# Delta-rule attention and two MLPs on one core: the second inverse gets its own buffers, the first is shared between GpSimdE and VectorE

## The chip, the cores and the metric

The kernel runs on one core of one Trainium2 chip. The metric is the device time of one execution in microseconds (us). The engines are named as in the profile: PE is TensorE (matmul), PEld its weight loads, DVE is VectorE, ACT is ScalarE, POOL is GpSimdE, and SP is SyncE, which in this kernel issues the DMAs.

## The reference, cut to what matters

```python
# attention: B, H, S, D = 4, 8, 768, 48; k_n = k / (norm(k) + 1e-6)
for t in range(S):
    y[:, :, t] = einsum('bhd,bhde->bhe', q[:, :, t], state)
    v_old = einsum('bhde,bhd->bhe', state, k_n[:, :, t])
    state = state + beta[t] * einsum('bhd,bhe->bhde', k_n[:, :, t], v[:, :, t] - v_old)
x = y laid out as (B*S, H*D) = (3072, 384)
# first MLP (384 -> 2048 -> 384), weights in float64
h = x @ w_in;  P = a0 + a1*h + a2*h^2 + a3*h^3;  Q = 1 + |b0|*|h| + |b1|*h^2
x = (P / (Q + 1e-6)) @ w_out
# second MLP, other weights
out = (max(x @ w_in2, 0)**2) @ w_out2
```

## The kernel before, in words

**Attention.** The 768 positions are cut into 12 chunks of 64. A step is one chunk of one batch (4 pairs of heads), and 8 steps (2 chunks x 4 batches) are a group: 6 groups. Inside a chunk the recurrence is solved with the inverse of a unit lower triangular matrix built from K^T K. For a whole group this is done at once, with 128 partitions that hold 32x32 blocks: the two diagonal blocks of each 64x64 matrix are inverted row by row (one multiply into `tmp`, one subtraction from `Tt`, for each of 31 values of s), and two small matmul stages (`m1`, `m2`) make the off-diagonal block. `Gb` holds the scaled K^T K, `Tt` the growing inverse, `TT` the finished 64x64 blocks, `TN` the transposed copies for the matmuls, `nbr` and `nrm` what comes from the norms and beta.

Groups 2 to 5 are inverted on POOL in rows of 32 (`st1` L504, `st2` L508), while the first MLP runs. Groups 0 and 1 take another way in the kernel before: 16x16 blocks on DVE (`st16`, L495 and L497, 15 values of s), and then a merge from 16 to 32 on PE (`ma` L565, `mb` L576, `mc` L587, with `me` L569 on DVE), through `Nb`, `Eb`, `DN`, `ident` and `half`. All groups share one `Gb` and one `Tt`, and K^T K of group 1 goes through DRAM (`gs`) to come back as `Gb`.

A step of the attention (L702, L761, L762) needs its mask on POOL (L740, one for each half of a tile `X`), copies on ACT and additions to the state on DVE.

**The MLPs.** They work on 512 tokens (two chunks) at a time: i = 0 to 5 in the first layer, then 6 again in the second. For each i there are 16 blocks j of the hidden layer: 9 matmuls with `Aw[j]` (L902, split into a high and a low part), the function on ACT, POOL (L922) and DVE, and 3 matmuls with `Bw[j]` (L938). The first i of layer 1 needs group 0 of the attention; group i+1 is done inside the time of i. The first layer's weights arrive as float64, 768 KB for each j, and are turned into float32 on ACT (L844) and DVE (L845, L846, L849, L851); ACT (L860) and POOL (L861) make the high and low parts of `Aw[j]`. DVE's and POOL's parts are once for each j.

**The order.** A planner (`Plan`) takes all tasks with assumed durations, due times and buffer pools, plays them through several times and keeps the best order. Each engine then executes its own list strictly in that order: an instruction that waits holds up all that stands behind it on its engine. `T0` is the planned time of the first MLP matmul, `inv_due` when the inverses are due. Matmuls on a tile `ones` fill planned gaps of PE. In the kernel before, SP issues all DMAs, weights too.

Of the kernel before, what the change touches and what calls it, by code (L numbers as in the profile page):

```python
# [48 lines left out]
class Plan:  # L49
# [13 lines left out]
    def add(self, eng, dur, fn, r=(), w=(), due=0.0, lock=0, alloc=None, free=(), kb=0, after=(), iss=0.35, nb=0.0):  # L63
# [179 lines left out]
def kernel(ctx, tc, kT, kS, qT, kn, vn, beta, par_in, w1, w2, outT):  # L243
# [117 lines left out]
    def eye():  # L361
        P_.memset(ident, 0.0)
        for o in range(0, 128, 32):
            P_.affine_select(ident[o:o + 32], ident[o:o + 32], pattern=[[1, 32]], base=0, channel_multiplier=-1,
                             compare_op=ALU.not_equal, fill=1.0)
    add("POOL", 1.0, eye, w=["ident"], due=15)

    def halves():
        P_.memset(half, 1.0)
        for o in range(0, 128, 32):  # L370
            P_.affine_select(half[o:o + 32], half[o:o + 32], pattern=[[0, 1]], base=-16, channel_multiplier=1, compare_op=ALU.is_ge, fill=0.0)
    add("POOL", 0.6, halves, w=["half"], due=5)
    add("POOL", 1.0, lambda: P_.memset(Nb, 0.0), w=[("N", o) for o in range(0, 128, 32)], due=3)
# [16 lines left out]
    def inv_due(g):  # L390
# [3 lines left out]
        if g == 1:  # L394
            return T0 - 10, T0 + 20
# [56 lines left out]
    def attention(g):  # L452
        d0, d1 = inv_due(g)
        if g:
            for n in range(8, 24) if g == 1 else ():
                dn = 8 + 1.5 * n if n < 16 else GD + 2 * (n - 16)
                gload(n, dn, 1.5 * n - 2 if n < 16 else GN + 2 * (n - 16))
                add("PE", 0.6, lambda n=n: [M.matmul(*y, start=True, stop=True) for y in gram(n)], r=[("kg", n)], w=[("G", n)], due=dn,  # L458
                    alloc=(("att", "h") if n < 16 else ("att",), ("G", n)), free=[("kg", n)])
# [625 lines left out]
```

## Time and profile before

| | before |
|---|---|
| median of 3 runs | 1114.44 us (1114.34 to 1118.63) |
| the profiled execution's own time | 1113.5 us |
| its span | 1111.8 us |
| PE busy | 1062.5 us (96%) |
| DVE / ACT / POOL busy | 693.9 / 658.6 / 396.9 us |
| mean granted clock of PE | 0.965 |

The span is what the profiler's rows cover; the execution's own time is 1.7 us longer. Rows give start, duration, engine, line and operation, and in brackets idle time of that engine just before and what ended it. A clock of 1.00 is PE at 2.4 GHz, 0.50 at 1.2 GHz.

### The profile page before, as it was taken

What the parts mean: (1) busy time and instruction counts of PE and PEld (TensorE: products, weight loads), DVE (VectorE), ACT (ScalarE), POOL (GpSimd) and SP (SyncE); (2) the same over time, 40 slices, a digit from 0 to 9 for tenths busy, and PEclk for the clock granted to TensorE, in tenths of its full rate; (3) what the DMA queues carried; (4) which work ended last, traced back from release to release, by engine and by line L of the source; (5) the groups of instructions that cost most, each with busy time, mean ns of one, the idle gap of its engine ahead of it and who ended that gap; (6) DMA issues with size and microseconds to landing.
All of it is one profiled execution on the core that took longest, in us unless ns stands there. A gap on an engine that the chain in (4) does not pass through costs nothing.

```text
span 1111.8 us, 24492 instructions
## 1 busy us (share of the span) xinstructions
PE 1062.5 (96%) x10014; PEld 757.8 (68%) x10014; DVE 693.9 (62%) x1116; ACT 658.6 (59%) x1193; POOL 396.9 (36%) x540
## 2 busy tenths in 40 slices
PE   6688999999999999999999899999999999999998
PEld 5576665556665666666666455688888888888887
DVE  4658988896667667766677599995333333333432
ACT  5265877877767777777878588754324242333422
POOL 6104699468528843972233153552000000000000
PEclk7577999999999999999999999999999999999999
DMA  7465336820640263033010220720001010000000
GB/s 234 103 174 160 70 99 191 219 67 23 158 93 33 74 154 83 13 95 83 29 28 12 90 85 29 240 101 29 29 0 57 1 48 10 1 29 1 29 1 29
DMA packets 116064, 83.48 MB, mean 75 GB/s; under 512 B 83568, under 2 KB 101104, under 8 KB 115952
## 3 DMA queue, kind: packets, MB, share of 16 engines
q1 hardware_dynamic: 115952, 81.92, 26.2%
q8 instruction: 79, 1.29, 0.5%
q14 instruction: 33, 0.27, 0.1%
HBM read 62.88 MB, written 17.83 MB: 73 GB/s over the span
## 4 chain that ended last, share of the span: by engine, by line
PE 84%; DVE 6%; POOL 4%; issue 3%; ACT 2%; DMA 1%; SPq 0%; POOLq 0%; ACTq 0%; DVEq 0%
PE bank L902 34%; PE bank L938 20%; PE bank L964 6%; PE bank L962 6%; PE bank L963 6%; PE bank L702 6%; PE bank L761 2%; POOL tmp L504 1%; POOL Tt L508 1%; PE bank L613 1%; PE bank L625 1%; DVE tmp L495 1%; POOL mem L922 1%; PE bank L458 1%; DMA mem<-in_w_dram 1%
## 5 line engine op out<-in xcount | busy, mean ns | idle before, releaser
L902 PE MATMUL bank<-xh,A 128*128 128x512 f32 x1152 | 360.1, 394 | 3.0 <-POOL A L861 3.0
L938 PE MATMUL bank<-mem,B 128*128 128x512 f32 x576 | 278.0, 615 | 1.3 <-DVE mem L929 1.3
L902 PEld LDWEIGHTS bank<-xh,A 128*128 128x128 f32 x1152 | 218.4, 190 | 62.6 <-issue 13.0
L902 PE MATMUL bank<-xl,A 128*128 128x512 f32 x576 | 254.2, 441 | 5.2 <-DVE mem L929 5.2
L922 POOL TENSOR_TENSOR mem<-mem 128x512 f32<-128x512 f32 x96 | 127.6, 1329 | 200.5 <-ACT mem L920 199.7
L938 PEld LDWEIGHTS bank<-mem,B 128*128 128x128 f32 x576 | 105.1, 192 | 98.8 <-issue 84.6
L950 DVE SCALAR_TENSOR_TENSOR mem<-bank,mem 128x512 f32<-128x512 f32 x96 | 66.1, 689 | 151.4 <-ACT mem L949 151.3
L949 ACT ACTIVATE mem<-bank 128x512 f32<-128x512 f32 x96 | 57.4, 598 | 152.8 <-PE bank L902 152.5
L902 PEld LDWEIGHTS bank<-xl,A 128*128 128x128 f32 x576 | 109.3, 190 | 43.6 <-issue 12.9
L964 PE MATMUL bank<-gh,C 128*128 128x512 f32 x288 | 113.9, 395 | 0.0
L962 PE MATMUL bank<-gl,C 128*128 128x512 f32 x288 | 113.6, 394 | 0.0
L963 PE MATMUL bank<-gh,C 128*128 128x512 f32 x288 | 112.1, 389 | 0.0
L953 DVE TENSOR_TENSOR gl<-mem,gh 128x512 fp32r<-128x512 f32 x96 | 71.5, 745 | 63.4 <-ACT gh L952 63.2
L952 ACT CAST gh<-mem 128x512 fp32r<-128x512 f32 x96 | 59.6, 620 | 74.9 <-DVE mem L950 61.9
L927 DVE SCALAR_TENSOR_TENSOR mem<-mem,par,bank 128x512 f32<-128x512 f32 x96 | 71.3, 743 | 51.6 <-ACT bank L926 51.4
L923 DVE TENSOR_TENSOR mem<-bank,mem 128x512 f32<-128x512 f32 x96 | 65.8, 686 | 39.8 <-ACT mem L347 38.7
L925 ACT ACTIVATE mem<-mem,par 128x512 f32<-128x512 f32 x96 | 69.4, 723 | 34.2 <-POOL mem L922 33.6
L920 ACT ACTIVATE mem<-mem,par 128x512 f32<-128x512 f32 x96 | 78.0, 813 | 2.5
L919 ACT ACTIVATE mem<-bank 128x512 f32<-128x512 f32 x96 | 56.9, 592 | 37.7 <-PE bank L902 37.0
L347 ACT COPY X<-bank 64x256 f32<-64x256 f32 (+1 forms) x189 | 63.7, 337 | 19.6 <-DVE vn L745 10.5
L924 DVE SCALAR_TENSOR_TENSOR mem<-mem,par,bank 128x512 f32<-128x512 f32 x96 | 71.6, 746 | 3.4 <-ACT mem L919 0.7
L504 POOL TENSOR_TENSOR tmp<-Gb,Tt 128x31 f32<-128x31 f32 (+15 forms) x124 | 67.0, 540 | 16.9 <-DVE Tt L489 8.5
(124 smaller groups left out, 1557.5 us busy)
## 6 DMA issues: line engine op xcount, KB each, us to landing
raw<-in_w_dram SPq DMA_DIRECT2D x18, 768.0 KB, 4.8
B<-in_w_dram SPq DMA_DIRECT2D x10, 768.0 KB, 4.8
kTg<-in_kS_dram SPq DMA_DIRECT2D x40, 128.0 KB, 2.8
gs<-Gs SPq DMA_DIRECT2D x40, 128.0 KB, 2.9
kTc<-in_kT_dram SPq DMA_DIRECT2D x40, 128.0 KB, 2.1
X<-in_qT_dram SPq DMA_DIRECT2D x96, 48.0 KB, 2.8
kn<-in_kn_dram SPq DMA_DIRECT2D x12, 384.0 KB, 4.0
vn<-in_vn_dram SPq DMA_DIRECT2D x12, 384.0 KB, 3.6
```

The lines of the kernel that those rows point to most:

```text
L504: P_.tensor_tensor(tv, _mid(Gb[:, s, s + 1:32], [128, a, b]), Tt[:, 0:a, s:s + 1].to_broadcast([128, a, b]), op=ALU.mult)
L902: M.matmul(h, a, b, start=(k == 0 and m == 0), stop=(k == NK - 1 and m == 2))
L920: add("ACT", 0.83, lambda: A_.activation(b(), a(), AF.Identity, bias=s(4), scale=s(5)), r=[ak, "par"], w=[bk], due=due + 3.3, alloc=(("b", ...
L922: add("POOL", 1.32, lambda: P_.tensor_tensor(b(), b(), a(), op=ALU.mult), r=[ak], w=[bk], due=due + 4.2, lock=1)
L924: add("DVE", 0.75, lambda: V.scalar_tensor_tensor(c(), c(), s(1), h(), op0=ALU.add, op1=ALU.mult), r=[hk, "par"], w=[ck], due=due + 6.3)
L925: add("ACT", 0.72, lambda: A_.activation(a(), b(), AF.Ln, bias=s(6)), r=[bk, "par6"], w=[ak], due=due + 6)
L927: add("DVE", 0.75, lambda: V.scalar_tensor_tensor(c(), c(), s(0), h(), op0=ALU.add, op1=ALU.mult), r=[hk, "par"], w=[ck], due=due + 8)
L938: M.matmul(acc[d], Bw[j][:, 128 * d:128 * d + 128], slot[gk], start=(j == 0), stop=(j == NJ - 1))
L953: add("DVE", 0.72, lambda: V.tensor_tensor(gl(), b(), gh(), op=ALU.subtract), r=[bk, gk, "late"], w=[lk], due=due + 5, lock=1, alloc=(("gl ...
L962: M.matmul(acc[d], wh, gl, start=(j == 0), stop=False)
L963: M.matmul(acc[d], wl, gh, start=False, stop=False)
L964: M.matmul(acc[d], wh, gh, start=False, stop=(j == NJ - 1))
```

## The change

Groups 0 and 1 are no longer done in blocks of 16 with a merge. Both use the row-by-row inverse of 32. For group 0, rows 0 to 2 of each block are computed on POOL and rows 3 to 31 on DVE, each with its own `tmp` (rows don't depend on each other). Group 1 is inverted wholly on POOL, as groups 2 to 5 are, and its result goes through DRAM as theirs does. There are two sets of `Gb` and `Tt`, so the second inverse doesn't wait for the buffers of the first. K^T K for steps 8 to 31 is done ahead of the first MLP (8 to 23 before), with four buffers each for load and store in place of two. The first layer's weights are asked for by ACT (`A_.dma_start`) in place of SP, and the planner starts them at 24 us and spaces them by 4.5 us. `T0` goes from 88 to 78.

```diff
-T0, U1, U2 = 88.0, 6.0, 4.15
+T0, U1, U2 = 78.0, 6.0, 4.15
-STEP0, STEP1, INV0, INV1 = 40, 25, -90, -10
-GD, GN = T0 + 10, 60
+STEP0, STEP1, INV0, INV1, LAZY = 40, 25, -100, -10, 0
+NEARLY, ROW0, WNB, WSTEP = 32, 3, 24, 4.5
+GD = 28
...
-    tmp = at.tile([128, 256], F32, name="tmp")
+    Gbs, Tts = ([at.tile([128, 32, 32], F32, name=f"{x}{i}") for i in range(2)] for x in ("Gb", "Tt"))
+    tmps = {x: at.tile([128, 256], F32, name=f"tmp{x}") for x in ("DVE", "POOL")}
...
-    tiles(at, "kTg", 2, [128, NP, C])
-    tiles(at, "Gs", 2, [128, NP, C])
+    tiles(at, "kTg", 4, [128, NP, C])
+    tiles(at, "Gs", 4, [128, NP, C])
...
         if g == 1:
-            return T0 - 10, T0 + 20
+            return 25, T0
...
-        either(0.35, 0.3, o1, r=[key], w=[("Dg", n)], due=n, free=[key])
+        add("ACT", 0.28, lambda f=o1: A_.copy(*f()), r=[key], w=[("Dg", n)], due=n, free=[key])
         for o in (32, 96):
-            either(0.33, 0.3, lambda o=o, f=o2: f(o), r=[key], w=[("TN", o)], due=n + 8, free=[key])
+            add("DVE", 0.28, lambda o=o, f=o2: V.tensor_copy(*f(o)), r=[key], w=[("G21", o)], due=n + 2, free=[key])
...
-            for n in range(8, 24) if g == 1 else ():
+            for n in range(8, NEARLY) if g == 1 else ():
...
-        for s in range(15 if g < 2 else 0):
...
-            add("DVE", 0.42 + 4.0e-3 * a * b, st16, r=GB, w=["Tt", "tmp"], due=d1, lock=1)
-        for s in range(31 if g > 1 else 0):
+        for s in range(31):
+            b = 31 - s
+            for E_, eng, lo, hi in ((V, "DVE", ROW0, s + 1), (P_, "POOL", 0, min(ROW0, s + 1))) if g == 0 else ((P_, "POOL", 0, s + 1),):
...
+                    E_.tensor_tensor(tv, _mid(Gb[:, s, s + 1:32], [128, a, b]), Tt[:, lo:hi, s:s + 1].to_broadcast([128, a, b]), op=ALU.mult)
...
+                    E_.tensor_tensor(Tt[:, lo:hi, s + 1:32], Tt[:, lo:hi, s + 1:32], tv, op=ALU.subtract)
...
-        for hf in range(2 if g < 2 else 0):
-            ka, kb, kc = ("mA", g, hf), ("mB", g, hf), ("mC", g, hf)
...
-            m = n + 16 if 0 < g < NG - 2 else None
+            m = n + 16 if NEARLY <= n + 16 < NSS else None
...
+        if l == 1:
+            add("ACT", 0.3, lambda: A_.dma_start(raw(rk), src[j]), w=[(rk, 0)], due=2 + 4.5 * j, alloc=None if e else (("raw",), rk), nb=WNB + WSTEP * j)
```

The order on POOL moves most. In the kernel before, this stands on POOL from the masks of steps 4 to 7 to the first function of the MLP (`X` masks, `vn` values times norms, `A_79` to `A_84` the low parts of `Aw[0]` to `Aw[5]`):

```order
L740 AFFINE_SELECT X_109<-X_109 64x4x64 x2
L657 TENSOR_TENSOR vn_130<-vn_130,nT_126 128x768
L539 MEMSET TT_112 32x32x32 x2
L740 AFFINE_SELECT X_110<-X_110 64x4x64 x2
L475 MEMSET Tt 128x1024
L861 TENSOR_TENSOR A_82<-mem,A_82 128x384
L657 TENSOR_TENSOR vn_131<-vn_131,nT_126 128x768
L861 TENSOR_TENSOR A_83<-raw_103,A_83 128x384
L922 TENSOR_TENSOR mem<-mem 128x512 x3
```

`A_79` to `A_81` stand ahead of this piece, and no inverse does. In the changed kernel the same place reads (`Gb_115`, `Tt_117`: group 1's own buffers):

```order
L485 TENSOR_TENSOR tmpPOOL<-Gb_115,Tt_117 128x87
L667 AFFINE_SELECT X_110<-X_110 64x4x64 x2
L489 TENSOR_TENSOR Tt_117<-Tt_117,tmpPOOL 128x29x3
L485 TENSOR_TENSOR tmpPOOL<-Gb_115,Tt_117 128x60
L489 TENSOR_TENSOR Tt_117<-Tt_117,tmpPOOL 128x30x2
L485 TENSOR_TENSOR tmpPOOL<-Gb_115,Tt_117 128x31
L489 TENSOR_TENSOR Tt_117<-Tt_117,tmpPOOL 128x31
L510 MEMSET TT_112 32x32x32 x2
L461 MEMSET Tt_116 128x1024
L792 TENSOR_TENSOR A_79<-mem,A_79 128x384
L792 TENSOR_TENSOR A_80<-mem,A_80 128x384
```

POOL's list up to here now holds 62 instructions for group 0's rows 0 to 2, then two `vn` and four masks, then group 1's 62 with the eight masks of steps 4 to 7 among the last 25 of them, then two kinds of memset, and only then `A_79`, which the first MLP matmul reads.

The second place is ACT at the start of the MLP. Before, from the last high part of the input to the first functions (L919, L920):

```order
L347 CAST xh_98<-xin 128x512
L347 COPY TT_112<-bank_75 32x16x32 x4
L919 ACTIVATE mem<-bank_73 128x512
L920 ACTIVATE mem<-mem,par 128x512
L347 ACTIVATE mem<-bank_73,par 128x512
```

And now (L850 and L851 are the same two functions, L505 the copy of group 1's inverse):

```order
L505 COPY Gb_115<-Tt_117 128x1024
L791 CAST A_85<-B 128x384
L791 CAST A_86<-B 128x384
L343 CAST xh_96<-xin 128x512
L343 CAST xh_98<-xin 128x512
L850 ACTIVATE mem<-bank_73 128x512
L757 DMA raw_103<-in_w_dram 128x768
L851 ACTIVATE mem<-mem,par 128x512
L757 DMA raw_104<-in_w_dram 128x768
L850 ACTIVATE mem<-bank_74 128x512
```

Two weight loads now stand between the functions; each waits until POOL and DVE have read the block that lay in its buffer before.

## Rows read from the trace of the kernel before

**Rows 1.** Stages: PE, PEld, DVE, ACT, POOL busy (count), PE clock, DMA, GB/s.

```profile
0.00:103.77 103.77, 74.14 (x2331) 63.99 (x2331) 66.57 (x140) 49.06 (x119) 33.80 (x62) 0.71 0.60 170
103.77:222.50 118.73, 111.91 (x1628) 71.97 (x1629) 100.31 (x163) 95.78 (x176) 84.76 (x110) 0.97 0.52 144
222.50:318.50 96.00, 94.24 (x988) 59.11 (x988) 71.74 (x122) 70.85 (x132) 62.08 (x94) 1.00 0.38 92
```

**Rows 2.** Timeline of PE: first value product, first MLP matmul of i = 0 and 1.

```profile
65.53 1.95 PE L702 MATMUL bank<-vn,TT 64*64 64x48 f32 x32
...
103.70 0.80 PE L902 MATMUL bank<-xl,A 128*128 128x512 f32 x1
...
224.93 0.50 PE L902 MATMUL bank<-xl,A 128*128 128x512 f32 x1
```

**Rows 3.** Timeline of DVE up to the end of the second inverse.

```profile
12.05 0.56 DVE L845 TENSOR_SCALAR mem<-mem 128x768 uint32<-128x768 uint32 x1 [12.05 <-DMA mem<-in_w_dram]
...
21.88 0.41 DVE L489 COPY Tt<-nbr 128x32 f32<-128x32 f32 x1
...
22.32 1.88 DVE L495 TENSOR_TENSOR tmp<-Gb,Tt 128x30 f32<-128x30 f32 x1
...
30.12 0.29 DVE L495 TENSOR_TENSOR tmp<-Gb,Tt 128x128 f32<-128x128 f32 x1
30.44 0.29 DVE L497 TENSOR_TENSOR Tt<-Tt,tmp 128x128 f32<-128x128 f32 x1
...
34.80 1.95 DVE L530 STREAM_TRANSPOSE Gb<-Tt 128x1024 f32<-128x1024 f32 x1
...
65.21 0.19 DVE L495 TENSOR_TENSOR tmp<-Gb,Tt 128x30 f32<-128x30 f32 x1
```

**Rows 4.** Timeline of SP, first load for group 1's K^T K.

```profile
14.16 0.33 SPq L332 DMA_DIRECT2D kTg<-in_kS_dram  x1
```

**Rows 5.** Timeline of POOL ahead of the first MLP.

```profile
22.68 1.47 POOL L657 TENSOR_TENSOR vn<-vn,nT 128x768 f32<-128x768 f32 x1
...
87.72 1.94 POOL L539 MEMSET TT<- 32x1024 f32 x2
...
93.67 1.05 POOL L861 TENSOR_TENSOR A<-mem,A 128x384 fp32r<-128x384 f32 x1 [1.23 <-ACT A L860]
```

**Rows 6.** Timeline of DVE beside the inverse of group 2 on POOL.

```profile
134.32 1.37 DVE L849 SCALAR_TENSOR_TENSOR raw<-raw 128x384 uint32<-128x384 uint32 x1
135.61 0.95 DVE L851 SCALAR_TENSOR_TENSOR B<-raw 128x384 uint32<-128x384 uint32 x1
...
189.46 0.55 DVE L849 SCALAR_TENSOR_TENSOR raw<-raw 128x384 uint32<-128x384 uint32 x1
```

**Rows 7.** Timeline of POOL: the inverse of group 2, and one pair of group 3's.

```profile
126.39 0.24 POOL L504 TENSOR_TENSOR tmp<-Gb,Tt 128x31 f32<-128x31 f32 x1 [0.19 <-DVE Tt L489]
...
135.23 0.92 POOL L508 TENSOR_TENSOR Tt<-Tt,tmp 128x192 f32<-128x192 f32 x1
...
180.49 0.59 POOL L508 TENSOR_TENSOR Tt<-Tt,tmp 128x192 f32<-128x192 f32 x1
...
338.01 0.34 POOL L504 TENSOR_TENSOR tmp<-Gb,Tt 128x87 f32<-128x87 f32 x1
338.43 0.35 POOL L508 TENSOR_TENSOR Tt<-Tt,tmp 128x87 f32<-128x87 f32 x1
```

**Rows 8.** Busy POOL by stage, line 504 alone: groups 2 and 3.

```profile
126.00:197.00 71.00, 20.16 (x31) 0.98 0.40 119
320.00:410.00 90.00, 15.61 (x31) 0.98 0.32 77
```

**Rows 9.** The same for line 508.

```profile
126.00:197.00 71.00, 18.45 (x31) 0.98 0.40 119
320.00:410.00 90.00, 16.79 (x31) 0.98 0.32 77
```

**Rows 10.** The same for the masks, line 740.

```profile
126.00:197.00 71.00, 8.00 (x14) 0.98 0.40 119
```

More of the change, by code (lines that the diff above doesn't have):

```diff
@@ L61, in pool, with add @@
         self.pools[name] = list(bufs)
-    def add(self, eng, dur, fn, r=(), w=(), due=0.0, lock=0, alloc=None, free=(), kb=0, after=(), iss=0.35, nb=0.0):
+    def add(self, eng, dur, fn, r=(), w=(), due=0.0, lock=0, alloc=None, free=(), kb=0, after=(), iss=0.35, nb=0.0, lazy=0.0):
         alt = None
@@ L359 @@
     add("POOL", 0.2, lambda: P_.memset(tiny, 1e-30), w=["tiny"])
[L361 to L373, printed above, removed]
     for b in range(B):
@@ L453, in attention @@
         d0, d1 = inv_due(g)
+        q = g % 2
+        Gb, Tt = Gbs[q], Tts[q]
+        gb, tt = (lambda o: ("Gb", q, o)), [("Tt", q, e) for e in ("DVE", "POOL")]
         if g:
-            for n in range(8, 24) if g == 1 else ():
[L456 to L459, printed above, removed]
+            for n in range(8, NEARLY) if g == 1 else ():
+                dn = 8 + 1.2 * n if n < 16 else GD + 1.1 * (n - 16)
+                gload(n, dn, 0.8 * n if n < 16 else 13 + 0.8 * (n - 16))
+                add("PE", 0.95, lambda n=n: [M.matmul(*y, start=True, stop=True) for y in gram(n)], r=[("kg", n)], w=[("G", n)], due=dn,
+                    alloc=(("att", "h"), ("G", n)), free=[("kg", n)])
                 gstore(n, dn)
@@ L474, in attention @@
         add("ACT", 0.25, lambda: A_.activation(nby, nby, AF.Exp, scale=0.5), r=["nby"], w=["nby"], due=d0)
-        add("POOL", 1.0, lambda: P_.memset(Tt, 0.0), w=["Tt"], due=d0)
+        add("POOL", 1.0, lambda: P_.memset(Tt, 0.0), w=tt, due=d0)
         def r1():
@@ L513, in attention @@
-        if g == 0:
-            add("ACT", 0.85, lambda: A_.mul(Nb.rearrange("r s p c -> r (s p) c")[:, :, 0:16], Dg.rearrange("r s p c -> r (s p) c")[:, :, 0:16], half),
-                r=[("Dg", n) for n in range(8)] + ["half"], w=[("N", o) for o in range(0, 128, 32)], due=d1)
-        elif g == 1:
-            for o in range(0, 128, 32):
-                c0 = o % 64
-                src = gs[g].rearrange("r s p c -> r (s p) c")[o + 16:o + 32, :, c0:c0 + 16]
-                dma(32, Nb[o + 16:o + 32, :, :, 0:16].rearrange("r s p c -> r (s p) c"), src, lat=2.5, iss=0.6,
-                    r=[("gs", 8 * g + ss) for ss in range(8)], w=[("N", o)], due=d1)
+        add("DVE", 0.25, lambda: V.tensor_copy(Tt.rearrange("p a b -> p (a b)")[:, 0:1024:33], nbr), r=["nbr"], w=tt, due=d0, lock=1)
@@ L544, in attention @@
         wT = [("TT", g % 2)]
-        for i in (1, 0) if g > 1 else ():
+        if g == 0:
+            for o in (32, 96, 0, 64):
+                either(1.1, 0.75, lambda o=o: (TTv[o:o + 32, :, o % 64:o % 64 + 32], Gb[o:o + 32]), r=[gb(o)], w=[("TD", o)], due=d1 + 5,
+                       after=[PL.last[wT[0]]])
+        for i in (1, 0) if g else ():
             for j in range(2):
@@ L720, in first @@
                 r += [("T", g % 2, k2 // 4, o) for o in (0, 64)] + [("vn", n2 // B % 2, k2 % B)]
-                r += [("TD", g, k2 // 4, o) for o in range(0, 128, 32)] if g < 2 else []
+                r += [("TD", o) for o in range(0, 128, 32)] if g == 0 else []
                 r += [("TTx", g % 2, i, j) for i in range(2) for j in range(2)] + ([("TT", g % 2)] if g < 2 else [])
@@ L828, in weights @@
         over = [i for k in (6, 7) if l == 1 and 4 * (k - 4) <= j < 4 * (k - 3) for i in used["raw", 1, k]]
-        dma(768 if f64 else 384, lambda: raw(rk), src[j], w=[rk, (rk, 1)], due=2 + 2 * j if e and l == 1 else d0 - 10, alloc=None if e else (("raw",), rk), lat=2.2, after=[used["load"]] + wait if l == 2 else [],
-            nb=0 if l == 2 else (3 + 7 * j if j < 3 else 44 + 4.5 * (j - 3)))
+        if l == 1:
+            add("ACT", 0.3, lambda: A_.dma_start(raw(rk), src[j]), w=[(rk, 0)], due=2 + 4.5 * j, alloc=None if e else (("raw",), rk), nb=WNB + WSTEP * j)
+            q = add("LAND", WSTEP - 0.5, lambda: None, r=[(rk, 0)], w=["wq"], due=d0 - 4)
+            add("LAND", 2.5, lambda: None, w=[rk, (rk, 1)], due=d0 - 2, after=[q])
+        else:
+            dma(768 if f64 else 384, lambda: raw(rk), src[j], w=[rk, (rk, 1)], due=d0 - 10, alloc=None if e else (("raw",), rk), lat=2.2, after=[used["load"]] + wait)
         if l == 1:
```

118 lines of the change are left out of this document (34 added, 84 removed).

## The prediction

> **What bounds the kernel now.** I read the stages first [rows 1]. From the first MLP matmul on, PE is busy nearly all the time (94.2 of 96.0 us in the second i), so the time after that point goes with PE's work. Ahead of it, PE is busy 74.1 of 103.8 us at a mean clock of 0.71, with small matmuls and fill: the prologue is a chain, not work. PE's timeline cuts the span [rows 2]: 103.7 us up to the first MLP matmul, 121.2 us for i = 0 (103.70 to 224.93), 886.9 us from there to the end at 1111.8. The second i takes 96 us [rows 1], so i = 0 holds some 25 us that PE alone doesn't ask for; there DVE is busy 100 of 119 us, and POOL 85. The change can win in these two places, and hardly in the last 887 us.
>
> In the prologue DVE and ACT wait for the first block of weights until 12.05; the scaled K^T K is ready at 22.3 (21.88 + 0.41); the inverse in blocks of 16 is over at 34.80 [rows 3]. The merge and the off-diagonal block then take until 65.5, when the first value product starts [rows 2]. Steps 0 to 7 and the merge of group 1 fill the other 38 us.
>
> **The change, part by part.** I follow POOL, since its list now carries the shared rows, the whole second inverse, the masks of steps 4 to 7 and `A_79`, one behind the other.
>
> *Start.* The 768 KB of weights no longer stand in front: nothing waits until 12.05 for them, and the loads of K for group 1, which follow at 14.16 [rows 4], come earlier. The chain of loads, Ln, Exp and scaling stays. I take 2.3 us off: the shared inverse starts at 20, not 22.3 (bounds: no gain, 22.3; all of the 12.05 less the 8 or so us that the other loads need, 18).
>
> *Shared rows.* Sizes follow from the loops. DVE has 28 values of s with 2 instructions, together 2 x 4060 elements a partition. Of 30 elements one takes 0.19 us, of 128 0.29, and the next starts 0.03 later [rows 3]: 0.16 + 0.00102 an element + 0.03. That is 56 x 0.19 + 8120 x 0.00102 = 18.9 us. POOL has 62 instructions with 2 x 1396 elements: 0.24 at 31, 0.34 to 0.35 at 87, steps of 0.42 at 87 [rows 7], so on average (45 elements) 0.27 and a gap of 0.08: 62 x 0.35 = 22 us.
>
> Do the two run side by side? In the trace they disturb each other. A DVE multiply of 30 elements takes 1.88 us while POOL multiplies for 1.47, and 0.19 with POOL quiet [rows 3, 5]. At 135 us two dense runs meet: DVE ends at 135.69, POOL at 136.15, DVE at 136.56 [rows 6, 7]. Each ends 0.41 to 0.46 after the other, though alone they take 0.55 and 0.59: they take turns, but some 0.13 of each overlaps with the other's turn. For the short instructions here (DVE 0.19 to 0.38, POOL 0.24 to 0.35) a turn is then 0.06 to 0.25, and most of it fits into the 0.2 us that the other engine needs to finish and start anyhow. A pair takes the longest of DVE's step, POOL's step and the sum of the two turns, about 0.4 in each case: 56 x 0.4 plus six single POOL instructions, 24 us. Bounds: 22 undisturbed, 41 if nothing overlaps (18.9 + 22). I take 24, nearer to the rows at 135. POOL is free at 44.
>
> The Trainium skill, "SBUF — State Buffer", section "Who interferes with whom", says that a VectorE instruction with both inputs in SBUF and a GpSimd instruction that reads SBUF block each other fully. By that rule taken literally the share would be the 41, not 24. The turns at 135 agree with the rule in kind, and show an overlap of 0.13 that it doesn't give.
>
> *Between.* Two `vn` of 1.47 [rows 5] and four masks with gaps, 0.5 each: 5 us, to 49. Group 1's scaled `Gb` must be there by then: its chain (load, matmul, copy, store, load) starts at about 12, and with four buffers each way I leave it 37 us. If it is later, all that follows on POOL moves with it.
>
> *Second inverse.* Group 3's, undisturbed by weight conversion, is 15.61 + 16.79 = 32.4 us busy [rows 8, 9], plus 62 gaps of 0.08: 37.4. Group 2's, beside the conversion of 8 blocks on DVE, is 20.16 + 18.45 = 38.6 busy, 6.2 more. In the changed kernel DVE converts 8 blocks in the same stretch, so 6.2 again (bounds: 3 if half of them come later, 12 if the denser run doubles it). The eight masks are 0.57 each with that disturbance [rows 10], 4.6, and 0.4 of gaps. 49 + 37.4 + 6.2 + 4.6 + 0.4 = 97.6.
>
> *To the first MLP matmul.* Two kinds of memset, 1.94 [rows 5] and half of that, then `A_79` 1.05 [rows 5]: 97.6 + 3.9 = 101.5. The last mask, 2 us before 97.6, leaves about as long a way (matmul, copy to `xin`, a DMA of 2 to 3 us, high part, low part): also near 102. So the first MLP matmul comes at **102**, against 103.7. DVE's way is shorter. From the end of the inverse to the first value product it took 31 us with the merge [rows 2, 3]; without it I give it half, so that product comes near 60 and the copies of step 4 near 70, while POOL reaches the masks of step 4 only after 43 of the 62 instructions, near 85. The time that the dropped merge frees is lost again on POOL. Bounds with the pieces above: 18 + 22 + 5 + 37.4 + 3 + 5 + 3.9 = 94, and 22 + 41 + 5 + 37.4 + 12 + 5 + 3.9 = 126, the latter only if everything goes wrong at once.
>
> *i = 0.* Out of this stage go the rest of group 1's merge on PE with its waits, its copies on DVE and ACT, K^T K of steps 24 to 31 and the conversion of 2 of 10 blocks on DVE. Group 1's result is there about 12 us after the first MLP matmul (its stores and loads through DRAM), 28 before, and POOL starts group 2's inverse 5 us after that matmul, not 23 (126.39 less 103.7) [rows 2, 7]. Nothing prices this directly. The bounds are 0 and the 25 us that this i has over the second; I take 9, since POOL still has about its 85 us of work here and DVE about 88 of its 100. New is that ACT waits in front of L851 for POOL to read `raw_103`: four `A` parts after the first, 4 us, of which some 2 show. That is within the 9. i = 0 takes **112**.
>
> *Sum.* 102 + 112 + 886.9 = 1101 us of span, plus 1.7 = **1103 us**, against 1113.5 of the profiled execution and a median of 1114.44.
>
> **The rivals.**
>
> 1. *Strict turns.* Without overlap the shared rows take 41, 17 more than I took. All of it goes to the start of the second inverse, because POOL is the chain: 1103 + 17 = **1120**, slower. For it: 1.88 us for a 0.19 us instruction [rows 3]. Against it: the overlap at 135. The change turns into a loss from a share of 41 on, and beyond 29 it wins less than 0.5%.
>
> 2. *POOL is quicker.* The share takes 22, the conversion costs 3, the start is at 18 and i = 0 is 8 shorter still, as its idle time and the late second group go: 94 + 106 + 886.9 + 1.7 = **1089**. For it: 25 us over the second i are a lot. Against it: DVE and POOL stay near 85% there.
>
> 3. *ACT waits for buffers.* Eight of the 16 weight loads now stand on ACT between functions of i = 0, each behind a part of `A` on POOL. If each holds ACT 1.2 us longer than the function can spare, i = 0 gives the 9 back: **1112**, no change. For it: ACT is busy 96 of 119 us in this stage [rows 1], and SP, where such waits were harmless, no longer takes them. Against: POOL's list has these parts in the order in which ACT asks.
>
> **How the numbers follow.** Chances: forecast 0.50, strict turns 0.14, POOL quicker 0.21, ACT's waits 0.15. The likeliest is 1103; its own range, from bounds that don't all fall together, is 1094 to 1111. Leaving out the outer half of the first two rivals gives 1088 to 1120. Half a per cent, 5.6 us, is about what tells this kernel from no change: faster is below 1109, which is most of the forecast and the quicker POOL, 0.64; same 0.21; slower, above 1120, 0.15.
>
> **What would show it.** Right: POOL without idle time from about 20 to 100 us; the first MLP matmul released by `A` on POOL or just behind it; masks of step 4 that wait for POOL and not for ACT; pairs of DVE and POOL in the share near 0.4 us. Wrong: the share over 30 us; the first MLP matmul before 95 or after 110; POOL idle before the second inverse (then its `Gb` came late, and loads are the chain); i = 0 longer than 118, with ACT idle behind L757.

## The result, and the profile after

The change made the kernel a little slower. The median is 1118.97 us (1114.31 to 1123.5, 20 runs) against 1112.65 for the kernel before (20 runs); the ratio is 1.0053, 95% interval 1.004 to 1.0067. The prediction was 1103. The profiled execution of the changed kernel took 1117.9 us, its span is 1116.2.

The same stages as in [rows 1], up to the first MLP matmul, i = 0, and 96 us of what follows (columns as there):

```profile
0.00:112.49 112.49, 79.58 (x1516) 68.18 (x1516) 74.88 (x163) 49.15 (x111) 84.42 (x171) 0.65 0.68 190
112.49:228.81 116.32, 105.32 (x1194) 66.11 (x1194) 98.94 (x157) 80.09 (x140) 92.17 (x117) 0.96 0.53 132
228.81:325.00 96.19, 94.18 (x924) 58.25 (x922) 70.15 (x116) 69.22 (x128) 63.78 (x94) 1.00 0.32 85
```

The timeline of PE has the three events of [rows 2] and one more, first value product, first MLP matmul of i = 0, 1 and 2:

```profile
71.00 2.80 PE L629 MATMUL bank<-vn,TT 64*64 64x48 f32 x48
...
112.49 0.50 PE L833 MATMUL bank<-xl,A 128*128 128x512 f32 x1 [0.73 <-DVE xl L817]
...
228.81 0.50 PE L833 MATMUL bank<-xl,A 128*128 128x512 f32 x1
...
330.72 0.80 PE L833 MATMUL bank<-xl,A 128*128 128x512 f32 x1
```

(The last row is the first matmul of i = 2.) The first MLP matmul comes 8.8 us later than before (103.70), i = 0 takes 116.3 instead of 121.2, and the rest 887.4 instead of 886.9: 8.8 - 4.9 + 0.5 = 4.4, the difference of the spans. So the change lost in the start, where it was made, and won about half of what I had put on i = 0.

The list of POOL, which the prediction followed, in the timeline (line 485 multiplies, 489 subtracts, 667 are masks, 510 and 461 memsets, 792 the low parts of `Aw`):

```profile
19.99 0.24 POOL L485 TENSOR_TENSOR tmpPOOL<-Gb,Tt 128x31 f32<-128x31 f32 x1
...
42.21 0.20 POOL L489 TENSOR_TENSOR Tt<-Tt,tmpPOOL 128x3 f32<-128x3 f32 x1
...
50.32 0.24 POOL L485 TENSOR_TENSOR tmpPOOL<-Gb,Tt 128x31 f32<-128x31 f32 x1 [3.25 <-issue]
...
84.61 0.41 POOL L667 TENSOR_SCALAR_AFFINE_SELECT X<-X 64x256 f32<-64x256 f32 x1 [3.32 <-ACT X L343]
...
106.37 0.27 POOL L489 TENSOR_TENSOR Tt<-Tt,tmpPOOL 128x31 f32<-128x31 f32 x1
106.70 1.95 POOL L510 MEMSET TT<- 32x1024 f32 x2
108.71 0.96 POOL L461 MEMSET Tt<- 128x1024 f32 x1
109.62 5.12 POOL L792 TENSOR_TENSOR A<-mem,A 128x384 fp32r<-128x384 f32 x4
```

The shared rows take 22.4 us (19.99 to 42.41). Then POOL stands 3.25 us. The row names no releaser, but group 1's `Gb` is only then scaled on DVE (L474 below, until 50.08). POOL runs the second inverse from 50.32 to 106.64, and stands 3.32 us in it for the masks of step 4. What came late shows on DVE and ACT:

```profile
38.24 0.24 DVE L485 TENSOR_TENSOR tmpDVE<-Gb,Tt 128x78 f32<-128x78 f32 x1
46.93 0.35 DVE L465 RECIPROCAL nbr<-nby 128x32 f32<-128x32 f32 x1 [8.45 <-ACT nby L460]
...
48.85 1.23 DVE L474 TENSOR_TENSOR Gb<-Gb,nbr 128x1024 f32<-128x1024 f32 x1
...
51.80 2.08 DVE L501 STREAM_TRANSPOSE Gb<-Tt 128x1024 f32<-128x1024 f32 x1
...
110.93 4.36 DVE L817 TENSOR_TENSOR xl<-xin,xh 128x512 fp32r<-128x512 f32 x3
```

```profile
45.81 0.37 ACT L343 COPY Gs<-bank 128x256 f32<-128x256 f32 x1 [5.16 <-DMA gs<-Gs]
46.29 0.35 ACT L459 ACTIVATE nby<-Gb,tiny 128x32 f32<-128x32 f32 x1
...
78.93 0.35 ACT L459 ACTIVATE nby<-Gb,tiny 128x32 f32<-128x32 f32 x1 [5.29 <-DMA Gb<-gs]
```

Group 1's scaling (L465) stands on DVE ahead of the last five instructions of group 0's inverse. DVE waits 8.45 us there, and group 0's inverse, near its end at 38.5, is over only at 51.7. Group 2's Ln (L459, 78.93) holds up the copies of the first steps in the same way. Behind both are DMAs. From 20 to 62 us the kernel before moved this,

```profile
DMA packets 9009, 5.50 MB, mean 131 GB/s; under 512 B 6707, under 2 KB 8387, under 8 KB 9000
gs<-Gs SPq DMA_DIRECT2D x7, 128.0 KB, 2.2
```

and the changed kernel this (KB each, median us from issue to landing):

```profile
DMA packets 11013, 10.69 MB, mean 255 GB/s; under 512 B 5171, under 2 KB 10054, under 8 KB 11007
mem<-in_w_dram ACTq DMA_DIRECT2D x4, 768.0 KB, 5.7
gs<-Gs SPq DMA_DIRECT2D x21, 128.0 KB, 4.5
kTg<-in_kS_dram SPq DMA_DIRECT2D x20, 128.0 KB, 5.1
```

Twice the bytes in the same stretch, and a store of `Gs` lands after 4.5 us, not 2.2.

### The profile page after: what moved, and what is told of

Its sections match the earlier page's. It is cut to its first block, busy times and chain, and to the rows that moved or that the text cites. A ratio compares the mean times of both kernels' runs of the same rounds, so it can differ in the third digit from the quotient of the medians.

```text
span 1116.2 us, 22110 instructions
## 1 busy us (share of the span) xinstructions
PE 1060.2 (95%) x8768; PEld 754.3 (68%) x8768; DVE 708.6 (63%) x1139; ACT 638.2 (57%) x1140; POOL 455.2 (41%) x653
## 4 chain that ended last, share of the span: by engine, by line
PE 75%; POOL 7%; DMA 6%; DVE 5%; ACT 3%; issue 2%; SPq 2%; POOLq 0%; ACTq 0%; DVEq 0%
PE bank L833 31%; PE bank L869 17%; PE bank L895 6%; PE bank L893 6%; PE bank L894 6%; PE bank L629 5%; POOL tmpPOOL L485 2%; DMA kTg<-in_kS_dram 2%; POOL Tt L489 2%; SPq L328 2%; PE bank L688 2%; DMA Gb<-gs 2%; POOL mem L853 1%; DMA gs<-Gs 1%; POOL X L667 1%
## 5 line engine op out<-in xcount | busy, mean ns | idle before, releaser
L833 PEld LDWEIGHTS bank<-xl,A 128*128 128x128 f32 x576 | 108.9, 189 | 46.9 <-issue 13.6
L485 POOL TENSOR_TENSOR tmpPOOL<-Gb,Tt 128x87 f32<-128x87 f32 (+25 forms) x186 | 98.7, 531 | 25.4 <-DVE Tt L475 9.0
L489 POOL TENSOR_TENSOR Tt<-Tt,tmpPOOL 128x87 f32<-128x87 f32 (+25 forms) x186 | 100.4, 540 | 13.2
L883 ACT CAST gh<-mem 128x512 fp32r<-128x512 f32 x96 | 59.6, 620 | 75.1 <-DVE mem L881 62.2
L850 ACT ACTIVATE mem<-bank 128x512 f32<-128x512 f32 x96 | 56.9, 593 | 48.8 <-PE bank L833 46.1
L851 ACT ACTIVATE mem<-mem,par 128x512 f32<-128x512 f32 x96 | 78.0, 813 | 2.3
```

The lines of the kernel that those rows point to most:

```text
L485: E_.tensor_tensor(tv, _mid(Gb[:, s, s + 1:32], [128, a, b]), Tt[:, lo:hi, s:s + 1].to_broadcast([128, a, b]), op=ALU.mult)
L489: E_.tensor_tensor(Tt[:, lo:hi, s + 1:32], Tt[:, lo:hi, s + 1:32], tv, op=ALU.subtract)
L833: M.matmul(h, a, b, start=(k == 0 and m == 0), stop=(k == NK - 1 and m == 2))
L851: add("ACT", 0.83, lambda: A_.activation(b(), a(), AF.Identity, bias=s(4), scale=s(5)), r=[ak, "par"], w=[bk], due=due + 3.3, alloc=(("b", ...
```

## The experiments

Each is an edit of the changed kernel; the ratio is to the kernel before, measured on the same chip. "Start" is the first MLP matmul of i = 0, "i = 0" the time from there to that of i = 1, both from the profiled execution, which can lie up to 5 us from the median of its kernel (those of e4 and x1 were their quickest, that of e5 nearly so). Line numbers shift by up to 2. In e5, y1, z1 and z2, and in x3 against e4, every engine's list is that of the kernel that was edited, but for the edit itself (z1: that of x1). In the other runs the planner laid out all lists anew, and a difference holds that reordering too.

| run | median us | ratio (95%) | start | i = 0 |
|---|---|---|---|---|
| changed kernel | 1118.97 | 1.0053 (1.004 to 1.0067) | 112.5 | 116.3 |
| e1, Ln of group 1 later | 1134.98 | 1.0169 (1.0145 to 1.0194) | 121.7 | 121.5 |
| e2, also Ln of group 2 later | 1132.83 | 1.0164 (1.014 to 1.0188) | 120.5 | 120.5 |
| e3, K^T K of 24 to 31 back | 1124.72 | 1.0085 (1.0067 to 1.0104) | 111.8 | 122.7 |
| e4, weights on SP | 1110.26 | 0.9952 (0.9934 to 0.9969) | 109.0 | 105.4 |
| e5, conversion left out | 1119.01 | 1.0035 (1.0022 to 1.0049) | 109.0 | 117.3 |
| e6, bytes counted | 1126.65 | 1.0118 (1.0101 to 1.0134) | 117.7 | 123.7 |
| e7, no rows shared | 1121.88 | 1.0068 (1.0054 to 1.0082) | 110.2 | 118.7 |
| e8, SP, inverse put behind | 1110.56 | 0.9962 (0.9949 to 0.9974) | 105.7 | 113.3 |
| x1, ACT early, SP late | 1111.04 | 0.9985 (0.997 to 0.9999) | 108.0 | 105.3 |
| x2, SP early, ACT late | 1120.97 | 1.0083 (1.0063 to 1.0103) | 110.6 | 117.7 |
| x3, SP, conversion left out | 1099.92 | 0.989 (0.9868 to 0.9912) | 101.2 | 104.7 |
| x4, SP, second inverse shared | 1115.87 | 1.0033 (1.0018 to 1.0049) | 108.8 | 114.4 |
| y1, Ln of group 3 later | 1120.79 | 1.0074 (1.0051 to 1.0097) | 113.3 | 117.1 |
| y2, third buffer | 1123.82 | 1.0103 (1.0078 to 1.0128) | 113.4 | 118.4 |
| y3, SP, third buffer | 1112.37 | 0.9998 (0.9984 to 1.0013) | 111.1 | 104.2 |
| z1, order for SP, ACT asks | 1111.05 | 0.9982 (0.9968 to 0.9996) | 111.7 | 105.4 |
| z2, order for ACT, SP asks | 1120.85 | 1.0057 (1.004 to 1.0074) | 112.0 | 119.9 |

### What holds up the start

My first theory (A) was that the waits in order seen above are the price.

```diff
# e1 (e2: nb=(0, 44, 78)[...]): the Ln of a group, in attention(g)
-        ... r=GB + ["tiny"], w=["nby"], due=d0)
+        ... r=GB + ["tiny"], w=["nby"], due=d0, nb=(0, 44, 0)[min(g, 2)])
# e3
-NEARLY, ROW0, WNB, WSTEP = 32, 3, 24, 4.5
+NEARLY, ROW0, WNB, WSTEP = 24, 3, 24, 4.5
# e4
-            add("ACT", 0.3, lambda: A_.dma_start(raw(rk), src[j]), w=[(rk, 0)], ...
+            dma(768 if f64 else 384, lambda: raw(rk), src[j], ..., nb=WNB + WSTEP * j)
```

e1: 

> One edit: the planner is told that group 1's Ln on ScalarE can't start before 44 us, so that the last steps of group 0's inverse stand ahead of group 1's scaling on VectorE. Theory A (waits in order): in the changed kernel VectorE stood 8.45 us in front of group 1's scaling with the last five instructions of group 0's inverse behind it. These now end near 40 us instead of 51.7, the first value product comes 4 to 8 us earlier than its 71 to 72, the masks of step 4 no longer keep GpSimdE waiting (3.3 us), the first MLP matmul comes at 107 to 109 instead of 112.5, the time falls by 3 to 5 us to about 1114. Rival B (GpSimdE's work alone): its second inverse starts at 50.3 as before and is just as disturbed, so the first MLP matmul stays within 1 us of 112.5 and the time within 2 us of 1119. Rival C (K^T K on TensorE): the products of group 0's off-diagonal block stand behind K^T K that waits for its loads until 58 us, so the first value product stays at 70 or later and the time doesn't move.

e2: 

> As the run before, and group 2's Ln not before 78 us, so that the copies of steps 0 to 3 on ScalarE don't stand behind it (it waited 5.29 us until 78.9 there). Theory A: another 3 to 5 us off the step chain, the masks of step 4 are ready for GpSimdE, its idle time between 50 and 107 goes, the first MLP matmul at 105 to 108, the time 1111 to 1114. Rival B: no more than the idle 3.3 us of GpSimdE can be won by both runs together: 1116 or more.

e3: 

> Only K^T K of steps 24 to 31 is put back beside steps 8 to 15; the rest of the change stays. Theory A holds that these eight round trips do not delay group 1's Gb (its own eight stand first in every list), so group 1's scaling still waits until 44 to 46 us; they free TensorE for the off-diagonal block 4 to 6 us sooner and let group 2's Gb land near 72 instead of 78. First MLP matmul 108 to 111; i = 0 pays 2 to 4 us for the eight products and stores; time 1116 to 1120, no clear difference. Rival C (early K^T K is the price): first MLP matmul before 106, time below 1113.

e4: 

> Only the weights of the first MLP are asked for by SyncE again, at the same times (24 us and every 4.5 us after); the planner then counts their bytes against the other loads, which it did not when ScalarE asked. Theory A: the same 768 KB blocks meet the same K^T K loads, so group 1's Gb lands at 44 to 47 us as before; but the planner now sees it coming late and puts group 1's scaling behind the end of group 0's inverse, and group 2's Ln behind the steps. So it should be as good as the run with both moved: 1111 to 1115, first MLP matmul 105 to 109. Rival D (ScalarE's queue itself is the price, by its waits for buffers in i = 0): the start is as now, 111 to 113, and i = 0 is 2 to 4 us shorter than its 116.3. Rival B: 1117 or more.

In e1 the steps of theory A came true: group 0's inverse ends near 40.5, the first value product moves from 71.0 to 65.7. But the time went up by 16 us. POOL's timeline says why:

```profile
47.49 0.96 POOL L461 MEMSET Tt<- 128x1024 f32 x1
62.39 0.24 POOL L485 TENSOR_TENSOR tmpPOOL<-Gb,Tt 128x31 f32<-128x31 f32 x1 [13.95 <-DVE Tt L475]
```

The scaling, now behind other work on ACT and DVE, let POOL start the second inverse 12.1 us later, and the first MLP matmul followed with 9.2. Steps that are 5 us earlier won nothing there, with POOL that much later, and e2 shows the same. So A's forecast fell in both. The start followed POOL's list (theory B), though B had not foreseen the delay either. What the waits of A cost by themselves these two runs don't show. e3 gives the early K^T K its due: without it for steps 24 to 31 the first value product comes at 62.2, but i = 0 pays 6.4 us, the planner's reordering included. e4 came near A's numbers. Group 0's inverse ends at 40.5 in it too, and group 1's scaling starts at 48.0, hardly later than the 46.9 of the changed kernel; its start is 3.5 us shorter. The larger part of its gain, 10.9 us, lies in i = 0, of which A said nothing.

### POOL's list, and what the planner knows

```diff
# e5: conversion of weight blocks j < 8 on DVE, three instructions of four
+        al, si_ = (slice(0, 8), slice(0, 8)) if small else (slice(0, 2 * DM), si)
-... V.tensor_scalar(lo(), lo(), 29, ...
+... V.tensor_scalar(lo()[:, al], lo()[:, al], 29, ...
# e6: in the planner's play()
+                if t["kb"]:
+                    dma = max(dma, s) + t["kb"] / 240.0
# e7
-NEARLY, ROW0, WNB, WSTEP = 32, 3, 24, 4.5
+NEARLY, ROW0, WNB, WSTEP = 32, 0, 24, 4.5
# e8: the edit of e4, and
-STEP0, STEP1, INV0, INV1, LAZY = 40, 25, -100, -10, 0
+STEP0, STEP1, INV0, INV1, LAZY = 40, 25, -100, -10, 20
```

e5: 

> Left out: three of VectorE's four conversion instructions of the first eight weight blocks work on 8 columns instead of 384 or 768 (and A is filled with ones, B with zeros), so that VectorE hardly touches SBUF beside the second inverse; the order on every engine is that of the changed kernel. Theory B (GpSimdE's list is the chain, and the conversion beside it costs more than the 6.2 us that the prediction took): lines 485 and 489 together are busy 33 to 36 us instead of 42.2, the second inverse ends 6 to 9 us earlier than 106.6, the first MLP matmul comes at 104 to 107 instead of 112.5, the time falls by 5 to 8 us to 1111 to 1114. Rival E (the steps are the chain: the masks come when the steps are ready, whatever GpSimdE does): the instructions get shorter, but GpSimdE stands idle for it in front of the masks, and the first MLP matmul stays at 110 or later.

e6: 

> ScalarE asks for the weights as in the changed kernel, but the planner counts their 768 KB a block against the other loads, as it does when SyncE asks. Theory F (what the weights on SyncE won, 8 to 9 us against the changed kernel, came from the planner knowing the load on the DMA engines): as good as with SyncE, 1108 to 1113, i = 0 near 106. Rival D (ScalarE's own queue costs it: weight requests stand between its functions): the first MLP matmul near 109, but i = 0 stays at 113 or more; 1115 to 1119.

e7: 

> No rows of the first inverse on GpSimdE (all 31 steps on VectorE), the rest as changed. By the prediction's sizes VectorE alone needs 62 x 0.19 + 10912 x 0.00102 = 22.9 us, measured shared 22.4. Theory B: GpSimdE is free 22 us sooner but group 1's Gb isn't scaled before 50, so its second inverse starts at 50 to 51 as before; no gain there and none lost: 1116 to 1121, the first MLP matmul within 2 us of 112.5. Rival G (the shared rows pay): group 0's inverse ends 4 to 8 us later than its 51.7, the value product and the masks of step 4 with it, 1122 to 1127.

e8: 

> Weights asked for by SyncE, and group 1's inverse put behind by 20 us of due time on GpSimdE (LAZY = 20), so that the masks of steps 4 to 7 and the low parts of the weights go ahead of what is left of it. Theory B: the steps no longer wait for GpSimdE, the first MLP matmul comes at 98 to 104 instead of 109; group 1's inverse ends as late as before or later, and as its result is wanted only some 12 us into i = 0 or later, i = 0 gets at most 4 us longer: 1100 to 1106. Rival H (the inverse is wanted at once): i = 0 gives all of it back, 1108 to 1112.

e5 prices the conversion beside the second inverse. Busy POOL on lines 485 and 489, first the changed kernel, then e5 (window, length, busy, count, clock, DMA share, GB/s):

```profile
50.20:106.75 56.55, 22.62 (x31) 0.65 0.61 163
50.20:106.75 56.55, 19.59 (x31) 0.65 0.61 163
```

```profile
51.70:98.15 46.45, 15.74 (x31) 0.59 0.68 193
51.70:98.15 46.45, 16.69 (x31) 0.59 0.68 193
```

42.21 against 32.43: the conversion costs POOL 9.8 us (32.4 is also what group 3 takes undisturbed, [rows 8, 9]). The inverse is over at 98.1 instead of 106.6. Yet the first MLP matmul comes at 109.0, only 3.5 us earlier, and the median doesn't move (the profiled execution was 4.8 us quicker than it). PE in e5, where group 0's off-diagonal block (L541, L553) stands behind the K^T K of group 3:

```profile
60.13 1.12 PE L444 MATMUL bank<-kTg 48*64 48x64 f32 x16 [2.15 <-DMA kTg<-in_kS_dram]
61.19 3.51 PE L541 MATMUL bank<-Gb,mem 32*32 32x32 f32 x122
...
71.75 2.80 PE L629 MATMUL bank<-vn,TT 64*64 64x48 f32 x48
```

From there eight steps follow until 109: a second chain, which ends 3.5 us before the first MLP matmul of the changed kernel. B had the size of the disturbance right, E the end. e7: without shared rows the start is 110.2, i = 0 118.7, and the ratio is 1.0068 against 1.0053, intervals overlapping; sharing the first inverse wins nothing that these runs can tell. e8: the start gained 3.2 us against e4, i = 0 gave back 7.9, the median is that of e4, as rival H said. e6 missed on all sides: counted, the bytes moved the second inverse to 58.5 and i = 0 became 123.7, so what SP won was not simply the planner's knowledge.

### The halves, and both chains at once

```diff
# x1 (x2 the other way round, j >= 8)
-        if l == 1:
+        if l == 1 and j < 8:
             add("ACT", 0.3, lambda: A_.dma_start(raw(rk), src[j]), ...
+        elif l == 1:
+            dma(768 if f64 else 384, lambda: raw(rk), src[j], ...
# x3: the edits of e4 and e5. x4: the edit of e4, and for group 1
-... if g == 0 else ((P_, "POOL", 0, s + 1),):
+... if g < 2 else ((P_, "POOL", 0, s + 1),):      # rows 0 to 7 on POOL, 8 to 31 on DVE
```

x1: 

> The first eight weight blocks are asked for by ScalarE as in the changed kernel, the last eight by SyncE. Theory D (in i = 0 a request that stands between ScalarE's functions goes out late, or sends two blocks ahead of the loads that the steps wait for): the start stays as in the changed kernel, first MLP matmul 111 to 114, and i = 0 falls from 116.3 to 105 to 110 us, as with all weights on SyncE; time 1108 to 1113. Rival J (what SyncE won in i = 0 came from the better start, with the steps 17 us earlier): i = 0 stays at 114 to 118, time 1116 to 1120.

x2: 

> The other half: the first eight blocks on SyncE, the last eight on ScalarE. Theory D: start as with all on SyncE (first value product 53 to 56, first MLP matmul 108 to 110), i = 0 113 to 118: 1114 to 1119. Rival J: start as said, i = 0 near 105: 1108 to 1112.

x3: 

> All weights on SyncE, and left out as in the earlier run: most of VectorE's conversion of the first eight blocks. Theory K (two chains end together ahead of the first MLP matmul: GpSimdE's list, and the steps behind the late off-diagonal block of group 0): SyncE's requests alone took the steps' delay away (109.0), leaving out the conversion alone took 8.5 us off GpSimdE's list (109.0); both together free both, so the first MLP matmul comes at 99 to 103, the second inverse busy for 32.5 and over by 93 to 96. Time 1100 to 1105 if i = 0 stays at 105 to 108. Rival: a third chain (the last step's copy, DMA and split) holds it at 106 or later.

x4: 

> All weights on SyncE, and rows 8 to 31 of group 1's inverse on VectorE too (GpSimdE keeps rows 0 to 7), as group 0's rows are shared. GpSimdE saves some 2 x 2300 elements of 2 x 5456, by the undisturbed rows 12 of its 32.5 us; VectorE gets 46 instructions, some 14 us, and had about 37 us idle ahead of the first MLP matmul. Theory B (GpSimdE's list is the chain where the steps are early): first MLP matmul 101 to 105 instead of 109, time 1103 to 1108. Rival L (taking turns at SBUF and VectorE's conversions, which now come later, eat it): 107 to 111, time 1109 to 1114.

x1 and x2 came out as theory D forecast: it is the last eight requests, as they are planned. With them on SP i = 0 takes 105.3 and 105.4, with them on ACT 116.3 and 117.7, whoever asks for the first eight. (By the medians the difference is 8 to 11 us.) x3 confirms the two chains: SP's requests or the missing conversion alone bring the start to 109.0, both together to 101.2, and the median to 1099.92. In x4 the second inverse is over at 91.3, 13 us sooner than in e4, and the start stays at 108.8. The waits of x4 from 55 to 108 us (total, times, longest):

```profile
ACT A L789 <- DVE mem L778: 8.4, 1, 8.4
...
PE bank L629 <- DVE vn L672: 7.3, 2, 6.9
```

DVE's list, with 46 instructions more, is late in POOL's place: rival L, though the time (1115.87) lies above L's 1114 as well. x3 took this work off DVE as well as its disturbance off POOL, so it doesn't tell the two apart.

### Why the late requests cost

```diff
# y1: the Ln of a group
+        ..., nb=113 if g == 3 else 0)
# y2 (y3: with the edit of e4)
-    tiles(one, "raw", 2, [128, 2 * DM], w1.dtype)
+    tiles(one, "raw", 3, [128, 2 * DM], w1.dtype)
# z1: planned as x1, issued by ACT
+            add("SP", 2.2, lambda: A_.dma_start(raw(rk), src[j]), ..., kb=768, ...)
# z2: planned as the changed kernel, the late half issued by SP
+            add("ACT", 0.3, lambda: (A_ if j < 8 else SY).dma_start(raw(rk), src[j]), ...)
```

y1: 

> The changed kernel, with group 3's Ln on ScalarE not before the time at which its Gb lands (15 us later in the list). If the 3.1 us that ScalarE stood there is what the late requests cost, i = 0 falls from 116.3 to 112 to 114 and the time by 2 to 4 us to 1115 to 1117. If ScalarE's waits for buffers are the cost, at most 2 us: 1117 to 1120.

y2: 

> The changed kernel (ScalarE asks) with a third buffer for the weight blocks (raw), so that a request finds its buffer read some 10 us before its place in ScalarE's list. If ScalarE standing in front of requests is the cost (four of them held it 1.0 to 1.4 us each in i = 0, some 5 us), i = 0 falls to 108 to 112 and the time to 1111 to 1115. If not: 1117 to 1120.

y3: 

> All weights on SyncE and the third buffer. SyncE's waits held nobody up, so the buffer can only bring the conversion forward, and that isn't what PE waits for there (1.2 us for the low parts): i = 0 at 103 to 106, the time within 2 us of the 1110 with two buffers. If it falls by 4 us or more, the buffer itself, not who waits for it, was the limit.

z1: 

> Planned as with the last eight requests on SyncE (the kernel with i = 0 of 105.3), so every engine's other work stands in that order, but those eight are issued by ScalarE at the same places. Theory M (the order is the cost): i = 0 at 105 to 109, what ScalarE waits for buffers being all that is lost, and the time 1110 to 1114. Theory N (ScalarE's own request is the cost): i = 0 at 113 to 118, 1118 to 1121.

z2: 

> The mirror: every engine's other work in the order of the changed kernel, planned with the requests on ScalarE, but the last eight issued by SyncE. Theory M: i = 0 stays at 113 to 117, the time 1116 to 1120. Theory N: i = 0 falls to 105 to 109, the time to 1109 to 1113.

The Ln that ACT waits for isn't the cost: y1 is no faster than the changed kernel. y2 isn't either, and y3 keeps i = 0 at 104.2 and wins nothing more; but with the third buffer the lists were reordered, so these two alone don't clear the buffers. z1 and z2 settle it for theory M: the order in which all other work was laid out costs the 8 to 11 us, not ACT's request. z1 and x1 have one order and differ in who asks: the ratios are 0.9982 and 0.9985. So do z2 and the changed kernel: 1.0057 and 1.0053. In the order made for SP, ACT can ask, with two buffers, and i = 0 takes 105.4; in the order made for ACT, SP's asking doesn't help (119.9, above M's 117 even).

```profile
111.71 0.50 PE L835 MATMUL bank<-xl,A 128*128 128x512 f32 x1 [1.12 <-DVE xl L819]
...
217.08 0.79 PE L835 MATMUL bank<-xl,A 128*128 128x512 f32 x1
...
324.62 0.80 PE L835 MATMUL bank<-xl,A 128*128 128x512 f32 x1
```

This is PE in z1, with the first MLP matmul of i = 0, 1 and 2. i = 0 doesn't keep all that it wins: i = 1 takes 107.5 us here and 105.9 in x1, 101.9 in the changed kernel and 98.9 before. The cause of this stays open. Two places show what differs in i = 0. ACT, changed kernel, then z1 (its L852 is L850):

```profile
125.99 0.90 ACT L775 ACTIVATE raw<-raw 128x768 f32<-128x768 f32 x1
129.97 0.35 ACT L459 ACTIVATE nby<-Gb,tiny 128x32 f32<-128x32 f32 x1 [3.08 <-DMA Gb<-gs]
...
133.80 0.58 ACT L850 ACTIVATE mem<-bank 128x512 f32<-128x512 f32 x1
```

```profile
128.45 1.19 ACT L343 ACTIVATE ws<-bank 32x512 f32<-32x512 f32 x2
129.67 0.92 ACT L777 ACTIVATE raw<-raw 128x768 f32<-128x768 f32 x1
130.69 0.60 ACT L852 ACTIVATE mem<-bank 128x512 f32<-128x512 f32 x1
```

And PE near the end of i = 0, changed kernel, then the same stretch in z1:

```profile
210.76 0.50 PE L833 MATMUL bank<-xl,A 128*128 128x512 f32 x1
214.39 1.21 PE L833 MATMUL bank<-xh,A 128*128 128x512 f32 x2 [3.14 <-POOL A L792]
215.40 0.63 PE L833 MATMUL bank<-xl,A 128*128 128x512 f32 x1
```

```profile
204.55 0.49 PE L835 MATMUL bank<-xl,A 128*128 128x512 f32 x1
205.54 0.73 PE L835 MATMUL bank<-xh,A 128*128 128x512 f32 x2 [0.50 <-POOL A L794]
206.12 0.39 PE L835 MATMUL bank<-xl,A 128*128 128x512 f32 x1
```

The fourth block is 3.1 us later (133.80 against 130.69; 0.8 of this is the later start), and the fifteenth waits 3.14 us for its low part on POOL where z1 waits 0.50. Up to the fifteenth block the changed kernel falls 5.4 us behind z1 (98.3 against 92.8 from the start of i = 0), and in the last two blocks 5.5 more. Which of the many places makes up how much of the rest stays open; y1 took the Ln away at the first of them, and the block was no earlier (135.04).

Of the versions that leave nothing out, e4, the change with all weights on SP, has the lowest ratio to the kernel before: 0.9952, 0.9934 to 0.9969. e8, x1 and z1 also lie just below 1.

## Why the prediction was wrong

The two steps that failed are the price of the second inverse (48.6 us, measured 56.3) and "DVE's way is shorter", which left POOL as the only chain. Of the 10.5 us that the start came late, the second inverse has 7.7, its later begin 1.3, and the way from it to the first MLP matmul 1.5. By the prediction's own bands the median, 1118.97, lies in "same" (0.21), outside the forecast's own 1094 to 1111. Two of its signs of being wrong came true: the first MLP matmul after 110, and POOL idle before the second inverse.

**Start and shared rows: right.** 20 was 19.99, 24 was 22.4. That the start came so close is in part luck: the scaled K^T K was ready at 18.7, and DVE began its rows at 18.86, while POOL had two masks ahead of its own. Rival 1 (strict turns, 41) is refuted; that the time came near its 1120 is chance. The Trainium skill, "SBUF — State Buffer", section "Who interferes with whom", says that a VectorE instruction with two SBUF inputs contends with a GpSimd instruction that reads SBUF, and that this contention is an exclusive lock. For these short instructions the trace disagrees with a lock over their whole length (22.4 us where POOL alone was put at 22); for the conversion it agrees in kind (9.8 us on 32.4).

**Between: right in length, wrong in what follows.** The 5 us were 4.7. `Gb` was not there, and POOL stood 3.25; this moved the second inverse from 49 to 50.3.

**Second inverse: the term that was mis-sized.** 48.6 us were 56.3: conversion 9.8 instead of 6.2 (e5), idle time for step 4's masks 3.8 where I had none, masks 5.4 instead of 4.6, and 0.5 less of gaps. My bound of 12 for the denser run held; I had taken the value of group 2, whose stretch was 71 us long, for one of 56.

**"DVE's way is shorter": wrong.** I wrote that the first value product comes near 60, the copies of step 4 near 70, and that POOL is the only chain. The first value product came at 71.0, and POOL's first mask of step 4, which waited for these copies, at 84.6. I had priced each transfer by the traffic of the kernel before and not asked what group 1's scaling holds up on DVE if it is late, though I had put that question for POOL. So a second chain ended 3.5 us short of the first (e5). Of the runs that removed one cause alone, e4 and e5 both stop at 109.0; only x3, which removed both, passes the 102 (101.2).

**To the first MLP matmul:** 3.9 were 5.9. The low parts of `x` on DVE (L817) run beside `Aw` on POOL (L792), three in 4.36 us, where the median of that line is 0.69 each, and PE waits for them, not for `A`. In all 112.5 for 102.

**i = 0: 112 were 116.3.** I took 9 us of gain, and 4.9 came. My upper bound was read wrongly: the 96 us of [rows 1] are the length of the window that I chose. In the kernel before, i = 1 runs from 224.93 to 323.79, 98.9 us, so the bound is 22 and not 25. Rival 3 priced the ACT requests at 9, near to the 8 to 11 measured, but through ACT's waits for buffers; z1 shows that it is the order. In the other order the gain in i = 0 is 16 (105.3 in x1), within either bound, though 7 of it are lost again in i = 1. Taking the early K^T K of steps 24 to 31 out costs i = 0 6.4 us (e3).

**Rest:** 886.9 was 887.4. The misses add to 10.5 + 4.3 + 0.5 = 15.3 us, which is a span of 1116.2 instead of 1100.9. Rival 2 (1089) fell with the start; its sum takes 6 us off i = 0, where its text says 8.

## What to carry to other kernels

Ahead of an event that everything waits for, count the chains that end near it: shortening one is worth no more than its lead over the next (e5: 8.5 us on POOL gave 3.5), and an engine that takes the work over can become the next one (x4). Where a change adds traffic, price the transfers at the new traffic and ask for each thing that comes late what stands behind its first reader on every engine. Where lists are planned, a moved instruction reorders everything else: test the instruction and the order apart, by issuing it from the other engine in an unchanged plan.

## What the runs showed of the hardware

With all other work in one order, it made no difference which engine asked for the last eight blocks: ratio 0.9985 with SP (x1) and 0.9982 with ACT (z1), 1.0053 with ACT (changed kernel) and 1.0057 with SP (z2). The Trainium skill, "DMA: Bandwidth & Descriptors", section "Issuing engines are not separate DMA queues", says that DMAs started by different engines run on the same 16 DMA engines; these four runs agree with it. The median 128 KB store of `Gs` landed after 2.2 us in a stretch with a mean of 131 GB/s (kernel before) and after 4.5 us in one with 255 (changed kernel).

Behind PE's wait of 3.14 us near the end of i = 0 the granted clock fell, in a stretch that z1 goes through at 1.00 (changed kernel, then z1; columns as in [rows 1]):

```profile
211.30:214.40 3.10, 0.01 (x1) 0.01 (x1) 3.10 (x5) 1.29 (x3) 3.04 (x2) 1.00 0.73 181
214.40:218.70 4.30, 4.30 (x10) 3.17 (x11) 2.87 (x5) 1.63 (x4) 1.02 (x1) 0.60 0.91 137
210.76:228.81 18.05, 13.64 (x116) 8.54 (x111) 14.47 (x25) 12.03 (x20) 8.63 (x9) 0.91 0.57 151
```

```profile
204.55:217.08 12.53, 12.03 (x160) 7.61 (x159) 12.21 (x20) 10.81 (x19) 8.37 (x11) 1.00 0.92 247
```

A mean of 0.60 is mostly the lower level, 1.2 GHz; from 218.7 on the clock is 1.00 again. The 14 matmuls of 128x512 behind the wait take 6.3 us in the changed kernel (214.39 to 220.66) and 4.7 in z1 (205.54 to 210.22), so PE lost some 1.6 us beyond the wait itself. This was seen at one place; no run tests whether the wait alone brings the clock down.
